# Issue order and planner numbers of a fused sliding-window attention and SiLU layer: loads booked at measured landing times, batch 1's k and q split, one copy moved to GpSimd

## Chip, cores and metric

One core of one Trainium2 chip. The time is device microseconds (us) of one execution. The span in the profile is about 1.8 us shorter than that time. The kernel before takes 323.43 us (median of three runs, 322.89 to 325.09). This is an already tuned kernel: TensorE is busy for 95% of the span, so the question is about 2 us in the first 60.

## The reference

Two stages, float32 in and out. Heads 0 to 3 look at the last 32 positions ("plain", p in the names below), heads 4 to 7 at every fourth of the last 128 ("dilated", d in the names).

```python
# q, k, v: (8, 8, 576, 64); w_in: (512, 2048); w_out: (2048, 512)
scores = scale * np.matmul(q, k.transpose(0, 1, 3, 2))
mask_plain = (rel >= 0) & (rel < 32)
mask_dil = (rel >= 0) & (rel < 32 * 4) & (rel % 4 == 0)
masks = np.stack([mask_plain if h < H // 2 else mask_dil for h in range(H)], axis=0)
attn = softmax(np.where(masks, scores, -1e9))            # cut: written out in the reference
x = np.matmul(attn, v).transpose(0, 2, 1, 3).reshape(B * S, H * D)   # 4608 x 512
h = x @ w_in
return (h * (1.0 / (1.0 + np.exp(-h)))) @ w_out
```

## The kernel before

The kernel computes batch after batch of attention on TensorE and puts the two matmuls of the second stage (h and y in the profile) between its pieces. The order of instructions is made while the kernel is being built, by a small planner: every piece of work is a step with an estimated duration on TensorE, estimated durations on VectorE or ScalarE, and a list of what it waits for. A step that reads loaded data waits for a landing time out of a table. The planner always takes a step that is ready by its own clock. On the chip each engine then takes its instructions in that order; where the table was wrong, TensorE stands in front of an instruction whose data aren't there, with ready work behind it.

```python
HOP = 0.12                      # from the end on one engine to the start on the next, us
# landing times by batch, us
AT_DIL = {0: 7.6, 1: 33.5, 2: 53.0}     # k, q for the "td" transposes (heads 4-7)
AT_PLAIN = {0: 11.0, 1: 33.5, 2: 53.0}  # k, q of heads 0-3
AT_VRAW = {0: 11.8, 1: 35.5, 2: 55.0}
AT_VP = {0: 14.3, 1: 45.0, 2: 58.0}
AT_REST = 16.0
AT_V1 = (17.6, 19.8)
AT_WIN = [18.5, 21.0, 23.5, 26.0]       # four chunks of w_in
AT_WOUT = [38.0, 40.5, 47.5, 50.0]      # four quarters of w_out
# ... cut
for f0 in range(0, DFF, FC):            # all these loads go through one queue, issued by GpSimd
    nc.gpsimd.dma_start(out=w_in16[:, :, f0 : f0 + FC], in_=wi[:, :, f0 : f0 + FC])
issue_nat(1, 0, H)                      # k and q of batch 1, all eight heads
issue_vraw(1)
for f0 in range(0, NFF, 4):
    if f0 == NFF // 2:
        issue_vp(1)                     # v of batch 1, behind two quarters of w_out
    nc.gpsimd.dma_start(out=w_out16[:, f0 : f0 + 4], in_=wo[:, f0 : f0 + 4])
# ... cut: best() gives a copy to VectorE or ScalarE, whichever the plan says ends it first
def best(dve, act):
    ends = {e: max(plan.now, plan.free[e]) + us for e, us in (("DVE", dve), ("ACT", act))}
    return ("DVE", dve) if ends["DVE"] <= ends["ACT"] else ("ACT", act)
# ... cut: one group of h, four matmuls for 128 columns of w_in
def l1(ring, f):
    h = (ps_x if ring == "x" else ps_h).tile([P, GT], F32, tag=ring, name=f"h_{g}_{f}")
    for c in range(HP):
        nc.tensor.matmul(h[:, :w], w_in16[:, c, f * P : (f + 1) * P], x_g[:, c],
                         start=(c == 0), stop=(c == HP - 1))
    # ... cut: tanh on ScalarE, then gT = (tanh + 1) * h on VectorE
```

The softmax here doesn't subtract the row's maximum and nothing guards it: scores larger than these inputs give would overflow.

## Time and profile before

| kernel before | |
|---|---|
| time, median of three | 323.43 us |
| span of the profiled run, mean granted clock | 321.2 us, 0.988 |
| TensorE busy | 304.2 us |
| of it between 20 and 40 us | 15.04 us, clock 0.84 |
| longest wait of TensorE after the start | 3.6 us, for k and q of batch 1, until 36.70 us |
| load booked for 33.5 us by the planner, landed | 36.57 us |

The names in the profile: td are the transposes of k and q of heads 4 to 7, nat is where k and q land, s are scores, av_p and av_d the products with v, h and y the two matmuls of the second stage. A group of h is four 256-column matmuls in the stage that matters here. The granted clock is the share of its full speed that TensorE was given; at 0.50 it runs at half speed. The prediction shows the lines.

### The profile page before, as it was taken

The page shows a single profiled execution, that of the slowest core. Times are in us where ns is not written, and L with a number is a line of the kernel's source. Part 1 is how long each engine was busy: PE and PEld are TensorE (multiplying, and loading weights), DVE is VectorE, ACT ScalarE, POOL GpSimd, SP SyncE. Part 2 cuts the span into 40 slices and gives each one's busy share as a digit, 9 for nine tenths or more (in the row PEclk, how much of TensorE's full clock was granted, in tenths as well). Part 3 has the DMA queues.
Part 4 walks back from the last instruction along what each step waited for, and adds up shares of the span by engine and source line. Part 5 has one row for each costly group of instructions (what it writes and reads, how often), then busy time and mean ns, then how long its engine had stood idle before and what let it go on. Part 6 is the DMA issues. An engine that isn't in the chain of part 4 may idle for free.

```text
span 321.2 us, 6143 instructions
## 1 busy us (share of the span) xinstructions
PE 304.2 (95%) x2402; PEld 156.4 (49%) x2402; DVE 198.6 (62%) x496; ACT 164.8 (51%) x299; POOL 54.0 (17%) x87
## 2 busy tenths in 40 slices
PE   1989599999999999999999999999999999999994
PEld 1658466555545444444454455445444444444442
DVE  7479488789878788753796578658651553255000
ACT  6557286677665365453654464556352453355111
POOL 8952624002700005004100410000000000000000
PEclk9998799999999999999999999999999999999999
DMA  7999999996999739998999799952270000100221
GB/s 89 152 194 192 197 191 192 194 214 126 161 208 207 144 94 156 210 209 183 181 216 185 157 183 156 261 123 70 69 166 33 34 35 33 65 35 0 78 87 65
DMA packets 106629, 44.51 MB, mean 139 GB/s; under 512 B 73320, under 2 KB 101992, under 8 KB 106600
## 3 DMA queue, kind: packets, MB, share of 16 engines
q0 software_dynamic: 48464, 19.92, 53.4%
q1 hardware_dynamic: 52952, 14.75, 25.5%
q10 hardware_dynamic: 5184, 9.44, 8.5%
q8 instruction: 19, 0.31, 0.4%
q14 instruction: 10, 0.08, 0.1%
HBM read 39.84 MB, written 18.28 MB: 181 GB/s over the span
## 4 chain that ended last, share of the span: by engine, by line
PE 83%; DMA 7%; POOL 3%; DVE 2%; ACT 2%; issue 1%; ACTq 0%; POOLq 0%
PE y L884 38%; PE h L851 36%; DMA nat<-in_q_dram 5%; PE s L599 3%; DMA vp<-in_v_dram 2%; PE av_d L646 2%; PE av_p L646 2%; DVE oD L650 1%; POOL nat L128 1%; PE td L505 1%; ACT ob L895 1%; ACT probs L608 0%; DVE probs L617 0%; PE ta L480 0%; POOL nat L117 0%
## 5 line engine op out<-in xcount | busy, mean ns | idle before, releaser
L884 PE MATMUL y<-w_out,gT 128*128 128x512 f16 x576 | 138.1, 379 | 0.0
L862 DVE SCALAR_TENSOR_TENSOR gT<-th,h 128x512 f16<-128x512 f32 (+1 forms) x160 | 98.9, 629 | 58.6 <-ACT th L860 58.3
L860 ACT ACTIVATE th<-h 128x512 f32<-128x512 f32 (+1 forms) x160 | 88.6, 556 | 80.6 <-PE h L851 73.3
L851 PEld LDWEIGHTS <-w_in 128*128 128x128 f16 x640 | 59.2, 99 | 54.0 <-issue 1.7
L884 PEld LDWEIGHTS <-gT 128*128 128x128 f16 x576 | 54.0, 98 | 60.0
L851 PE MATMUL h<-xR,w_in 128*128 128x512 f16 x320 | 77.2, 379 | 0.2 <-DVE gT L862 0.2
L851 PE MATMUL h<-xA,w_in 128*128 128x512 f16 (+1 forms) x320 | 66.9, 345 | 0.6 <-ACT probs L612 0.6
L608 ACT ACTIVATE probs<-s 128x768 f16<-128x768 f32 (+2 forms) x46 | 36.0, 782 | 21.6 <-PE s L599 19.9
L895 ACT ACTIVATE ob<-y 128x512 f32<-128x512 f32 x36 | 21.5, 597 | 41.8 <-PE y L884 41.7
L650 DVE TENSOR_TENSOR oD<-av_d,rcps 72x256 f16<-72x256 f32 x64 | 26.9, 421 | 2.2
L646 PEld LDWEIGHTS <-probs 128*128 128x128 f16 x448 | 21.7, 99 | 13.2 <-DVE probs L617 1.4
L650 DVE TENSOR_TENSOR oP<-av_p,rcps 96x256 f16<-96x256 f32 x48 | 20.2, 421 | 1.6
L384 POOL COPY fence<-kqT 128x1 f16<-128x1 f16 x10 | 1.8, 190 | 95.4 <-DMA kqT<-kq_s 95.4
L617 DVE TENSOR_TENSOR probs<-probs,mask_p 128x768 f16<-128x768 f16 x21 | 11.6, 554 | 8.4 <-ACT probs L608 8.4
L646 PE MATMUL av_d<-vd,probs 128*128 128x65 f16 x256 | 14.5, 198 | 0.5 <-DVE oD L650 0.3
L617 DVE TENSOR_TENSOR probs<-probs,mask_d 128x576 f16<-128x576 f16 (+1 forms) x23 | 11.9, 516 | 4.0 <-ACT probs L608 3.0
L646 PE MATMUL av_p<-vp,probs 128*128 128x65 f16 x192 | 13.1, 194 | 0.7 <-ACT probs L612 0.5
L649 DVE RECIPROCAL rcps<-av_d 72x4 f32<-72x4 f32 x64 | 11.0, 171 | 3.3 <-PE av_d L646 3.1
L649 DVE RECIPROCAL rcps<-av_p 96x4 f32<-96x4 f32 x48 | 8.3, 174 | 7.3 <-PE av_p L646 6.8
L163 POOL DMA_DIRECT2D vraw<-in_v_dram x16 | 10.8, 678 | 8.6 <-DVE gT L862 2.2
L176 POOL DMA_DIRECT2D vp<-in_v_dram x7 | 10.0, 1428 | 3.9 <-PE h L851 1.8
L522 PE MATMUL td<-ident,xR 96*128 96x96 f16 x8 | 1.9, 276 | 6.8 <-DMA xR<-in_q_dram 6.8
(96 smaller groups left out, 158.7 us busy)
## 6 DMA issues: line engine op xcount, KB each, us to landing
out_dram<-ob ACTq DMA_DIRECT2D x36, 256.0 KB, 2.0
kq_s<-in_k_dram POOLq DMA_DIRECT2D x5, 576.0 KB, 10.7
kq_s<-in_q_dram POOLq DMA_DIRECT2D x5, 576.0 KB, 13.2
vp<-in_v_dram POOLq DMA_DIRECT2D x7, 384.0 KB, 8.5
w_in<-in_moe_w_in_dram POOLq DMA_DIRECT2D x4, 512.0 KB, 9.9
w_out<-in_moe_w_out_dram POOLq DMA_DIRECT2D x4, 512.0 KB, 14.1
vraw<-in_v_dram POOLq DMA_DIRECT2D x8, 224.0 KB, 5.9
x_s<-oP SPq DMA_DIRECT2D x10, 144.0 KB, 2.6
```

What stands on the lines that cost most here:

```text
L163: nc.gpsimd.dma_start(out=vraw[p0 : p0 + m1 - m0, ab].rearrange("p h r d -> p h (r d)"), in_=src[m0:m1],)
L176: nc.gpsimd.dma_start(out=vps[b % NV][:, :, :D], in_=v_win(b * H * S - W, HN * NB, QB * D))
L608: nc.scalar.activation(p2, both[:, :, :n], AF.Exp, scale=scale)
L617: nc.vector.tensor_tensor(p2, p2, mk, ALU.mult)
L646: nc.tensor.matmul(a[:, i, : D + 1], lhs(i), rhs(i), start=True, stop=True)
L649: nc.vector.reciprocal(rcp[:n], a[:n, :, D : D + 1])
L650: nc.vector.tensor_tensor(o, a[:n, :, :D], rcp[:n, :, None].broadcast_to([n, HN, D]), ALU.mult)
L851: nc.tensor.matmul(h[:, :w], w_in16[:, c, f * P : (f + 1) * P], x_g[:, c], start=(c == 0), stop=(c == HP - 1),)
L860: nc.scalar.activation(th[:, :w], h[:, :w], AF.Tanh, scale=0.5)
L862: nc.vector.scalar_tensor_tensor(gTs[g][:, f, :w], th[:, :w], 1.0, h[:, :w], ALU.add, ALU.mult)
L884: nc.tensor.matmul(y, gTs[g][:, f, tb * P : (tb + 1) * P], w_out16[:, f], start=(f == 0), stop=(f == NFF - 1),)
L895: nc.scalar.activation(ob, y, AF.Copy, scale=0.5)
```

## The change

The intent: the planner is told when loads land on the chip and how long instructions really take from start to start, so that it doesn't order work behind data that are late. The landing times now come from a running sum over the order of issue, so order and table can't drift apart. Four parts:

- **Loads.** Order and landing times come from one list. k and q of batch 1 are split, heads 4 to 7 (d1) first. The v load of batch 1 (v1) goes one place earlier, ahead of the second quarter of w_out. The new table books d1 for 32.5 us, p1 for 36.2, w_in for 21.15 to 28.8, w_out for 40.15 to 50.4; the times booked for batches 0 and 2 change too.
- **GpSimd copy.** One copy of v (batch 0, second half) moves from ScalarE to GpSimd (c0).
- **Lean.** The copies of batch 0 go to ScalarE if VectorE would end less than 0.3 us sooner.
- **Costs.** HOP and the estimated durations change by 0.01 to 0.12 us, and the step that copies v no longer names VectorE as its engine.

```diff
+    ORDER = "k0 r0 v0 w0 w1 c0 w2 w3 d1 p1 r1 o0 v1 o1 o2 o3".split()
+    LOAD_US = {"w": 2.55, "o": 2.55, "d": 3.7, "p": 3.7, "r": 1.4, "v": 2.6, "k0": 0.9, "r0": 1.2, "v0": 2.0, "c0": 0.0}
+    AT_W0 = 14.5
 ... (the fixed issues of before are taken out)
+    at = AT_W0
+    for what in ORDER:
+        kind, n = what[0], int(what[1:])
 ... (w, o, k0, r0, v0 issue the loads of before)
+        elif what == "c0":
+            nc.gpsimd.tensor_copy(vds[0][:, 1, :, :, :D], vraws[0][:, 1])
+        elif kind == "d":
+            issue_nat(n, HN, H)
+        elif kind == "p":
+            issue_nat(n, 0, HN)
 ... (r, v)
+        at += LOAD_US[what if n == 0 and kind in "krvc" else kind]
+        AT[what] = at
-    HOP = 0.12
+    HOP = 0.18
+    LEAN = 0.3
-    AT_DIL = {0: 7.6, 1: 33.5, 2: 53.0}
+    t2 = at
+    AT_DIL = {0: 6.7, 1: AT["d1"], 2: t2 + 7.0}
 ... (the other tables in the same way)
-    AT_WIN = [18.5, 21.0, 23.5, 26.0]
-    AT_WOUT = [38.0, 40.5, 47.5, 50.0]
+    AT_WIN = [AT[f"w{n}"] for n in range(4)]
+    AT_WOUT = [AT[f"o{n}"] for n in range(4)]
-            return ("DVE", dve) if ends["DVE"] <= ends["ACT"] else ("ACT", act)
+            return ("DVE", dve) if ends["DVE"] + LEAN * (b == 0) <= ends["ACT"] else ("ACT", act)
-            step = best(0.44, 0.58)
+            step = best(0.37, 0.58)
 ... (a dozen more durations in the same way)
+            if b == 0 and ab == 1:
+                return                     # this copy of v is GpSimd's
```

More of the change, by code (lines that the diff above doesn't have):

```diff
@@ L202 @@
     issue_vp_first(0)
-    issue_part(k, MA, M, nat_of(0, "rest"), 0, H)
-    issue_vraw(0, (1,))
-    issue_vp_first(1)
     nc.vector.tensor_scalar(band, band, 1.0, BIG, ALU.subtract, ALU.mult)
@@ L224 @@
     wi = moe_w_in.rearrange("(c p) f -> p c f", p=P)
-    for f0 in range(0, DFF, FC):
-        nc.gpsimd.dma_start(out=w_in16[:, :, f0 : f0 + FC], in_=wi[:, :, f0 : f0 + FC])
     wo = moe_w_out.rearrange("(c p) m -> p c m", p=P)
-    issue_nat(1, 0, H)
-    issue_vraw(1)
-    for f0 in range(0, NFF, 4):
-        if f0 == NFF // 2:
-            issue_vp(1)
-        nc.gpsimd.dma_start(out=w_out16[:, f0 : f0 + 4], in_=wo[:, f0 : f0 + 4])
+    AT = {}
+    at = AT_W0
+    for what in ORDER:
+        kind, n = what[0], int(what[1:])
+        if kind == "w":
+            nc.gpsimd.dma_start(
+                out=w_in16[:, :, n * FC : (n + 1) * FC], in_=wi[:, :, n * FC : (n + 1) * FC]
+            )
+        elif kind == "o":
+            nc.gpsimd.dma_start(
+                out=w_out16[:, 4 * n : 4 * n + 4], in_=wo[:, 4 * n : 4 * n + 4]
+            )
+        elif what == "k0":
+            issue_part(k, MA, M, nat_of(0, "rest"), 0, H)
+        elif what == "r0":
+            issue_vraw(0, (1,))
+        elif what == "v0":
+            issue_vp_first(1)
+        elif what == "c0":
[4 more added lines that the diff above has]
+            issue_nat(n, 0, HN)
+        elif kind == "r":
+            issue_vraw(n)
+        else:
+            issue_vp(n)
+        at += LOAD_US[what if n == 0 and kind in "krvc" else kind]
+        AT[what] = at
     def third_batch():
@@ L317 @@
     plan = Plan()
-    AT_DIL = {0: 7.6, 1: 33.5, 2: 53.0}
-    AT_VRAW = {0: 11.8, 1: 35.5, 2: 55.0}
-    AT_PLAIN = {0: 11.0, 1: 33.5, 2: 53.0}
-    AT_VP = {0: 14.3, 1: 45.0, 2: 58.0}
-    AT_CAST = 64.0
-    AT_REST = 16.0
-    AT_V1 = (17.6, 19.8)
-    AT_WIN = [18.5, 21.0, 23.5, 26.0]
-    AT_WOUT = [38.0, 40.5, 47.5, 50.0]
+    t2 = at
+    AT_DIL = {0: 6.7, 1: AT["d1"], 2: t2 + 7.0}
+    AT_PLAIN = {0: 11.3, 1: AT["p1"], 2: t2 + 7.0}
+    AT_VRAW = {0: 12.2, 1: AT["r1"], 2: t2 + 8.6}
+    AT_VP = {0: 14.5, 1: AT["v1"], 2: t2 + 11.4}
+    AT_CAST = t2 + 18.0
+    AT_REST = AT["k0"]
+    AT_V1 = (max(AT["r0"] + 1.2, 18.0), AT["v0"])
+    AT_WIN = [AT[f"w{n}"] for n in range(4)]
+    AT_WOUT = [AT[f"o{n}"] for n in range(4)]
     readers = {}
@@ L487, in trans_a @@
             ):
-                step = best(us + 0.04, us)
+                step = best(us, us)
                 yield step
@@ L495, in trans_b @@
                 nc.tensor.transpose(tps[:, r], pairs["q"][:, hp, r], ident[:MA, :MA])
-            step = best(0.44, 0.40)
+            step = best(0.47, 0.40)
             yield step
@@ L525, in trans_d0 @@
                     )
-            step = best(0.41, 0.52)
+            step = best(0.40, 0.52)
             yield step
@@ L555, in trans_a0 @@
                         )
-            step = best(0.55, 0.48) if nm == "k" else best(0.76, 0.68)
+            step = best(0.47, 0.42) if nm == "k" else best(0.68, 0.56)
             yield step
@@ L614, in scores @@
                 return
-            yield "DVE", 0.12 + n / 960
+            yield "DVE", 0.07 + n / 960
             mk = mk.rearrange("p a c -> p (a c)")[:, None, :].broadcast_to([P, 2, n])
@@ L619, in paired @@
         def paired(key):
-            step = best(0.42, 1.0)
+            step = best(0.335, 0.95)
             yield step
@@ L633, in vd_of @@
         def vd_of(ab):
-            step = best(0.42, 1.0) if pe_path else ("DVE", 0.42)
+            if b == 0 and ab == 1:
+                return
+            step = best(0.335, 0.95) if pe_path else ("DVE", 0.335)
             yield step
@@ L647, in av @@
             n = o.shape[0]
-            yield "DVE", 0.50
+            yield "DVE", 0.545
             nc.vector.reciprocal(rcp[:n], a[:n, :, D : D + 1])
@@ L691, in x_p @@
             dst = x_b[:, : HP // 2, QB * j : QB * (j + 1)]
-            step = best(0.22, 0.30)
+            step = best(0.17, 0.22)
             yield step
@@ L705, in x_d @@
             for hp in range(HP // 2):
-                step = best(0.40, 0.40)
+                step = best(0.365, 0.36)
                 yield step
@@ L792, in attention @@
             elif kind == "V":
-                st = Step(lambda ring, a=a: vd_of(*a), 0.0, (), [AT_V1[0] if b == 0 and a[0] else at_vraw], ("DVE",))
+                st = Step(lambda ring, a=a: vd_of(*a), 0.0, (), [AT_V1[0] if b == 0 and a[0] else at_vraw], ())
             elif kind == "P":
@@ L860, in l1 @@
             nc.scalar.activation(th[:, :w], h[:, :w], AF.Tanh, scale=0.5)
-            yield "DVE", 0.11 + w / 960
+            yield "DVE", 0.06 + w / 960
             nc.vector.scalar_tensor_tensor(
```

## The prediction

> **What bounds the kernel now.** I read the page first: busy shares, the 40 slices, the list of groups.
>
> ```profile
> PE 304.2 (95%) x2402; PEld 156.4 (49%) x2402; DVE 198.6 (62%) x496; ACT 164.8 (51%) x299; POOL 54.0 (17%) x87
> ...
> PE   1989599999999999999999999999999999999994
> ...
> PEclk9998799999999999999999999999999999999999
> ```
>
> TensorE is busy 95% of the span. The holes are in slices 1, 3 and 5 (8.03 us each), the last one at the tail, and in two of the slices between 16 and 40 us the granted clock drops as well. So I looked at who TensorE waited for, then at stretches of 20 us.
>
> ```profile
> PE td L522 <- DMA xR<-in_q_dram: 6.8, 1, 6.8
> PE td L505 <- DMA nat<-in_q_dram: 3.6, 1, 3.6
> ...
> PE h L851 <- ACT probs L612: 0.6, 1, 0.6
> PE av_p L646 <- ACT probs L612: 0.5, 1, 0.5
> ```
>
> ```profile
> 20.00:40.00 20.00, 15.04 (x151) 12.59 (x151) 13.44 (x41) 10.31 (x27) 8.35 (x11) 0.84 1.41 197
> 40.00:60.00 20.00, 19.40 (x247) 12.67 (x245) 17.41 (x57) 13.99 (x36) 5.40 (x7) 0.99 1.86 189
> ...
> 80.00:100.00 20.00, 20.00 (x181) 9.86 (x179) 16.53 (x43) 12.27 (x21) 6.04 (x9) 1.00 1.54 186
> ```
>
> The columns are the stretch, its length, then busy time of PE, PEld, DVE, ACT and POOL, the granted clock, the DMA share and GB/s. From 80 us on TensorE is full (20.00 of 20.00), and later stretches lose 0.2 us in all until the tail. Nothing can be won there by waiting less. The first 6.75 us precede any change. What is left is 20 to 62 us: 4.96 us idle up to 40 us, 0.6 us up to 60 us and 0.3 us after it. The timeline of TensorE shows the one large hole, and stretches cut at the holes show the clock (the figure after POOL's).
>
> ```profile
> 32.94 0.21 PE L505 MATMUL td<-ident,nat 96*128 96x96 f16 x1
> 36.70 0.93 PE L505 MATMUL td<-ident,nat 96*128 96x96 f16 x11 [3.56 <-DMA nat<-in_q_dram]
> 37.43 1.05 PE L851 MATMUL h<-xA,w_in 128*128 128x256 f16 x4
> ```
>
> ```profile
> 23.20:26.70 3.50, 3.47 (x31) 2.85 (x32) 3.09 (x11) 1.60 (x5) 0.98 (x2) 0.51 1.25 206
> 26.70:33.20 6.50, 6.45 (x60) 5.57 (x58) 6.10 (x17) 5.54 (x16) 2.56 (x3) 1.00 1.64 182
> 33.20:36.70 3.50, 0.00 (x0) 0.03 (x1) 0.34 (x1) 0.32 (x1) 1.18 (x3) 1.00 1.44 197
> 36.70:40.30 3.60, 3.60 (x33) 3.06 (x34) 2.39 (x7) 1.02 (x2) 2.59 (x4) 0.53 1.27 209
> ```
>
> The hole is the wait for k and q of batch 1 (all eight heads), which the kernel planned for 33.5 us and which landed at 36.57 us by the chain of waits. Behind it the granted clock is 0.50 until about 40.2 us: four 256-column matmuls take 0.85 us from start to start there, and 0.46 us in the run from 26.2 to 33 us. The same happens from 23.2 to 26.7 us, behind three short holes (0.63, 0.50, 0.28 us).
>
> **What the Trainium skill says.** "TensorE: Matmul & The Clock Gate", part 1, says that the clock halves after an idle window of some 3.4 us of a free-running counter and comes back after a busy one. The trace agrees in size: 0.50 for about 3.5 us, twice. The first time no single hole is 3.4 us long, so a window that is only partly busy is enough here (1.4 us idle of about 3.4). "GPSIMD Engine Reference", section 4.1, calls one-input copies on GpSimd roughly line-rate, and section 1 gives 1.2 GHz: an estimate of 1024 / 1.2 GHz = 0.85 us, with overhead about 1 us, for the moved copy of 128x1024. The trace before has no GpSimd copy of that size; ScalarE took 1.05 us for it and VectorE 0.41 to 0.53 us. Section 1 there also says that GpSimd shares its SBUF interface with VectorE; no run so far shows what that costs here.
>
> **The change, part by part.** I compared the instruction lists of the two builds.
>
> (1) Loads. GpSimd issues the same bytes in nearly the same order: four w_in chunks, k and q of batch 1, v, w_out. But k and q of batch 1 are split: heads 4 to 7 (which the td transposes need) come first, in four issues, heads 0 to 3 in another four. Four more issues at about 0.7 us each (the nat issues took 0.63 to 0.84 us) on a GpSimd that was waiting on landings anyway: no cost on the path. The queue drains in order: w_in chunk 3 lets a GpSimd issue go at 29.51 us, the q load lands at 36.57. With half the bytes the first half lands about half way, 29.4 + 3.6 = 33.0 us, the second about 36.6 us. w_out has the same bytes ahead of it as before, so its quarters land as now: issued at 26.42, 29.51, 33.47, 36.36 with 13.3 to 14.5 us to landing, so about 40.5, 43.5, 47.5 and 50.7 us; one v load now comes ahead of the second, which moves that to about 45.5.
>
> (2) What TensorE does before td. In the old order 18 groups of four h matmuls precede td, in the new one 14. Those four take 4 x 0.46 = 1.8 us, so TensorE comes to td at 33.0 - 1.8 = 31.2 us if all else stays, and up to 32.3 us if the early stage is worse by a microsecond. It then waits for 33.0. The hole shrinks from 3.56 to between 0.7 and 2 us, and td itself starts at about 33.1 instead of 36.7. The gain is 3.6 us minus the 1.8 us of h matmuls that now come afterwards, so 1.8 us, plus what is saved in clock.
>
> (3) Clock. If the hole is short enough, the half-speed stretch behind it goes: 3.5 us at half speed are 1.75 us of work lost. I give that even odds. So 1.8 to 3.5 us at this point.
>
> (4) What limits that gain. From td to the fourth quarter of the first y tile the new order holds 24 td transposes (1.0 us), 18 h groups (8.1), six score sets (1.8), the other transposes (1.6), 32 av matmuls (1.6) and three y quarters (2.6): 16.7 us of TensorE. 33.0 + 16.7 = 49.7 us, but the last w_out quarter lands at 50.7 us, so it starts at about 51.2 us, with the clock penalty or without. Before, this quarter starts at 52.66 us with one h group and one score set (0.75 us) fewer behind it. So 53.4 - 51.2 = 2.2 us.
> VectorE is the check: from the first td copy to the last gT of group 1 the new list has 19 gT (6.6 us by their spacing of 0.345), seven normalisations (3.8), mask products (2.1), transposed copies (3.5), pair copies and the rest (1.5): 17.5 us. From 33.3 us that ends at 50.8, or about 53 with the idle time of before; it ended at 55.8 before. So VectorE allows 2 to 3 us too.
>
> (5) The small parts. The first copies lean to ScalarE: three of the four td copies go there, but ScalarE has its eight L221 copies until 7.84 us, so the scores of batch 0 start about 0.2 us later. The GpSimd copy of v takes 1.05 us from ScalarE at 19.08 us, at a time when w_in is already queued well ahead: it delays the next w_in issue to about 18 us, and that chunk's turn in the queue comes at 23.9. An h group now stands ahead of a score set at about 20 us and will wait there for the first w_in chunk (at 21.0 us), about 1 us instead of 0.63; the av wait on ScalarE stays at about 0.5 us. All of this lies ahead of the wait at td and is swallowed by it, unless it comes to over 0.8 us. I book it at zero.
> (6) New costs in the planner only change interleaving later on, where TensorE is full. Zero, give or take 0.5 us.
>
> Sum: 323.43 - 2.2 = 321.2 us.
>
> **The rivals.** (a) The hole only moves: TensorE waits at td, then for w_out, and VectorE (17.41 busy of 20 us between 40 and 60 us) becomes the bound; the new plan gives it more of the ta copies (1.5 us). For it: VectorE is nearly full from 45.5 to 55 us already (9.10 of 9.50). Against it: it was idle from 33.5 to 37.2 us and need not be. It makes 322.5 to 323.5. (b) Both half-speed stretches vanish and all holes close: 5.9 us idle and 3.5 us of clock, 9.4 us at most, 314 us. Against it: w_out's landing at 50.7 us, which the change doesn't bring forward, and the first w_in chunk at 21 us. Even a part of it, say 4 us, needs loads that land earlier than now. (c) The GpSimd copy holds up the queue, because it waits for its v load and all loads behind it wait too. GpSimd reaches it at about 15.4 us; its load had landed by 16.8, since the issue at 16.78 needed that landing. If it took 4 us instead of 1, the queue would still hold w_in until 23.9. It makes 321.5 to 323.
>
> **Range and chances.** The three ways to the gain give 1.8, 2.2 and 2 to 3 us; rival (a) takes it to 0.5, the better clock to 3.5 to 4. With the scatter of the runs before (322.89 to 325.09) I take 319.6 to 322.8. Faster by over 2% means below 316.96 us, 6.5 us of the 9.4 that exist at all: 0.03. Slower by over 2% would need a new stall of 6 us in a stage that is full: 0.01.
>
> **What would show it.** Right: td of batch 1 starts at about 33 us behind a hole of 0.7 to 2 us; the fourth y quarter starts at about 51.2 us; from 80 us on TensorE is full as before and all is shifted by about 2 us; GpSimd's copy takes about 1 us and no w_in chunk lands later. Wrong: k and q of heads 4 to 7 land at 35 us or later (the split issues cost queue time), or holes of over 1 us appear between 40 and 60 us behind VectorE (then rival (a)), or the clock stays at 1.00 throughout and the time is below 319.6 (then the y quarter was not bound by w_out).

## The result, and the profile after

Four runs each: 320.23 us (319.8 to 321.11) against 323.36 us. Ratios here are the mean time of one kernel's fast runs over the mean of the other's fast runs in the same rounds, which isn't quite the ratio of the medians; this one is 0.9897, 95% interval 0.9855 to 0.9939. A second set on another chip, 14 runs against 61, gives 320.08 against 322.28 us, ratio 0.9937 (0.9913 to 0.9961): 2.0 to 2.2 us. That set is the better one, and I use it below. The changed kernel is faster, by less than 1%.

The page of the changed kernel (busy times; then TensorE and its granted clock in 40 slices of 7.99 us):

```profile
PE 303.2 (95%) x2402; PEld 155.7 (49%) x2402; DVE 197.0 (62%) x493; ACT 164.3 (51%) x300; POOL 58.2 (18%) x92
...
PE   1969989999999999999999999999999999999994
...
PEclk9975999999999999999999999999999999999999
```

The hole of slice 5 is gone. The hole of slice 3 has stayed, and the clock of the slice behind it has fallen to half. The waits of TensorE (what waited for what: us in all, times, longest) say the same:

```profile
PE td L546 <- DMA xR<-in_q_dram: 6.9, 1, 6.9
PE h L877 <- DMA w_in<-in_moe_w_in_dram: 2.8, 1, 2.8
PE y L910 <- DMA w_out<-in_moe_w_out_dram: 0.6, 2, 0.4
```

The 3.6 us for k and q of batch 1 are gone (td waits 0.2 us once, at 59.20 us, for batch 2). In their place the first group of h now waits 2.8 us for the first w_in chunk; before, it waited 0.6 us, for ScalarE. The timeline of TensorE (start, us, instruction, in brackets the idle time ahead of it) shows where:

```profile
18.74 0.30 PE L623 MATMUL s<-kqD 64*128 64x72 f16 x8
21.81 1.03 PE L877 MATMUL h<-xA,w_in 128*128 128x256 f16 x4 [2.77 <-DMA w_in<-in_moe_w_in_dram]
...
34.45 0.68 PE L529 MATMUL td<-ident,nat 96*128 96x96 f16 x12
42.38 1.02 PE L910 MATMUL y<-w_out,gT 128*128 128x512 f16 x4 [0.40 <-DMA w_out<-in_moe_w_out_dram]
...
52.67 1.02 PE L910 MATMUL y<-w_out,gT 128*128 128x512 f16 x4
```

td starts at 34.45 us with no wait, against 36.70. The last two lines are the first and the fourth quarter of the first y tile; each quarter needs its own quarter of w_out. Now the stretches (length; busy PE, PEld, DVE, ACT, POOL; granted clock; DMA share; GB/s), first those of the prediction, then two around the new hole:

```profile
20.00:40.00 20.00, 17.37 (x176) 13.91 (x177) 13.30 (x41) 10.47 (x29) 11.62 (x17) 0.74 1.29 181
40.00:60.00 20.00, 18.59 (x229) 11.93 (x229) 17.78 (x60) 12.66 (x30) 5.67 (x8) 1.00 1.53 198
80.00:100.00 20.00, 20.00 (x192) 10.12 (x189) 16.89 (x42) 13.48 (x24) 8.11 (x11) 1.00 1.40 170
```

```profile
16.80:20.20 3.40, 2.13 (x40) 1.20 (x39) 1.73 (x6) 2.37 (x6) 3.40 (x6) 1.00 1.24 184
20.20:30.50 10.30, 8.07 (x68) 5.75 (x69) 4.82 (x17) 3.43 (x10) 3.06 (x6) 0.50 1.30 201
```

Between 20 and 40 us TensorE is busy 2.3 us longer than before, but at a clock of 0.74 instead of 0.84: ten microseconds at half speed, against 3.5 and 3.6 before. Busy time and work are two things here. To compare work I counted, for several moments of each trace, which matmuls had yet to start, and took 0.216 us for one of 512 columns, 0.109 for 256 and 0.035 for the small ones. It is an estimate from the traces' own spacings at full clock. Work still to do, us:

| at (us) | before | changed, 1st profile | changed, 2nd profile |
|---|---|---|---|
| 33 | 273.8 | 277.0 | 274.7 |
| 40 | 272.2 | 270.7 | 269.2 |
| 62 | 252.6 | 251.5 | 249.7 |
| 100 | 215.7 | 214.2 | 212.2 |
| span | 321.2 | 319.4 | 317.4 |

The changed kernel comes to 33 us behind the old one (by 3.2 and 0.9 us of work): it stood in front of w_in and ran cold. It overtakes between 33 and 40 us, where the old one stood for 3.6 us and then ran at half speed. From 40 us on it leads by 1.1 to 1.5 us in one profile and by 2.9 to 3.5 in the other.

What holds TensorE from there on is w_out. The issues of its four quarters (first and last start) and the time from issue to landing, in the first profile:

```profile
L235 POOL DMA_DIRECT2D w_out<-in_moe_w_out_dram x4: 749/772/780, 33.5 to 37.1; - x4
DMA to landing us min/median/max: 8.8/12.6/15.3
```

By the trace's landing events the quarters are there at 42.34, 47.38, 49.96 and 52.48 us. The first quarter of y starts at 42.38, after a wait of 0.40 us, the second at 47.43, after 0.23. From there it is 5.24 us of TensorE to the fourth, which starts at 52.67 without a wait, but only 0.19 us after its load. In the kernel before, the last quarter of w_out had landed at 50.86 us, and TensorE came to it at 52.66, 1.8 us late. TensorE keeps the order that it was given: had it been faster ahead of 42 us, it would only have waited longer for the first quarter. So neither the hole at w_in nor the cold stretch behind it reached the end here.

### The profile page after: what moved, and what is told of

It is laid out like the page before. It is cut to its first block, busy times and chain, and to the rows that moved or that the text cites. A ratio compares the mean times of both kernels' runs of the same rounds, so it can differ in the third digit from the quotient of the medians.

```text
span 319.4 us, 6150 instructions
## 1 busy us (share of the span) xinstructions
PE 303.2 (95%) x2402; PEld 155.7 (49%) x2402; DVE 197.0 (62%) x493; ACT 164.3 (51%) x300; POOL 58.2 (18%) x92
## 4 chain that ended last, share of the span: by engine, by line
PE 82%; DMA 10%; POOL 4%; DVE 1%; issue 1%; ACT 0%; POOLq 0%
PE y L910 37%; PE h L877 36%; DMA nat<-in_q_dram 5%; PE s L623 3%; DMA w_out<-in_moe_w_out_dram 3%; DMA w_in<-in_moe_w_in_dram 3%; PE av_d L672 2%; PE av_p L672 2%; POOL vp L188 1%; POOL nat L131 1%; POOL vraw L166 1%; DVE oD L676 0%; POOL xR L131 0%; PE td L529 0%; PE xp L714 0%
## 5 line engine op out<-in xcount | busy, mean ns | idle before, releaser
L632 ACT ACTIVATE probs<-s 128x768 f16<-128x768 f32 (+2 forms) x47 | 36.2, 771 | 12.8 <-PE s L623 10.2
```

The costliest lines, as they stand in the source:

```text
L632: nc.scalar.activation(p2, both[:, :, :n], AF.Exp, scale=scale)
```

## The experiments

Twelve runs in three calls (the first is the changed kernel again); runs of one call share a chip and the runs of the kernel before. Where an edit is "to the changed kernel" it is that kernel plus the lines shown. All gave the right result, and all profiled runs were fast ones. The theory on record at the start was that of the prediction; the rivals were the clock, the GpSimd copy, and a hole that only moves.

| run | median us (runs) | ratio to before (95%) |
|---|---|---|
| after_again | 320.08 (14) | 0.9937 (0.9913 to 0.9961) |
| loads_only | 320.30 (22) | 0.9947 (0.9926 to 0.9968) |
| costs_only | 321.80 (22) | 0.9984 (0.9965 to 1.0004) |
| no_pool_copy | 320.26 (16) | 0.9928 (0.9903 to 0.9953) |
| before, first call | 322.28 (61) | |
| warm_hole | 318.99 (9) | 0.9916 (0.9883 to 0.9950) |
| warm_both | 318.86 (6) | 0.9899 (0.9864 to 0.9934) |
| no_split | 320.13 (10) | 0.9942 (0.9912 to 0.9973) |
| w0_early | 320.38 (13) | 0.9941 (0.9915 to 0.9966) |
| before, second call | 322.45 (25) | |
| td_time_only | 323.53 (22) | 1.0049 (1.0028 to 1.0070) |
| times_only | 323.61 (21, of them 6 slow, which the ratio leaves out) | 1.0018 (0.9994 to 1.0042) |
| no_lean | 320.21 (22) | 0.9955 (0.9934 to 0.9976) |
| warm_no_pool | 319.76 (22) | 0.9936 (0.9917 to 0.9955) |
| before, third call | 322.26 (73) | |

### The changed kernel once more

No edit.

> The changed kernel once more, for another profile and for the spread. Its first profile showed half clock from 20.2 to 30.5 us (mean clock 0.984) while three other executions had 0.989 to 0.995 and were only 0.8 to 1.3 us shorter. Theory L (loads: the weights' landing caps the early stage): the span stays between 318 and 319.5 us whatever the clock, and with a better clock there are longer waits for loads. Theory C (the clock phase is the gain): span follows the clock one to one, about 3 us between clock 0.984 and 0.995. Ratio to before expected 0.990.

Measured: 320.08 us, and a second profile (span 317.4 us). Its timeline at the same places:

```profile
21.20 0.61 PE L877 MATMUL h<-xA,w_in 128*128 128x256 f16 x4 [2.52 <-DMA w_in<-in_moe_w_in_dram]
...
31.78 0.93 PE L529 MATMUL td<-ident,nat 96*128 96x96 f16 x12
40.35 1.02 PE L910 MATMUL y<-w_out,gT 128*128 128x512 f16 x4 [0.66 <-DMA w_out<-in_moe_w_out_dram]
...
50.59 1.02 PE L910 MATMUL y<-w_out,gT 128*128 128x512 f16 x4
```

Nearly the same hole, 2.5 us, stands in front of w_in, but here the clock stayed down for a much shorter time: over 20 to 33 us it was 0.87, against 0.61 in the first profile. td starts 2.7 us earlier (0.6 of that because the first w_in chunk let TensorE go earlier), and the fourth y quarter 2.1 us earlier. It is tempting to put the 2.1 us down to the clock. But the loads differ as well:

```profile
L235 POOL DMA_DIRECT2D w_out<-in_moe_w_out_dram x4: 747/751/774, 31.8 to 35.5; - x4
DMA to landing us min/median/max: 8.5/12.2/15.0
```

The quarters of w_out landed at 40.30, 45.31, 47.87 and 50.53 us, each 2.0 to 2.1 us earlier than in the first profile. In both profiles TensorE waits for the first (0.66 us here) and the second (0.31, until 45.35), and the fourth y quarter starts 5.24 us later (here 0.06 us after its own load). Nothing shows that TensorE delayed them: the queue was 0.6 us apart at the first w_in chunk, 1.1 at the fourth and 1.4 at the first k load of batch 1 (31.31 and 29.91 us), and the next issue came 0.55 us after that landing in both. So the 2.1 us are those of the loads, and what the clock cost ahead of them was taken up by the waits. The waits grew from 0.6 to 1.0 us with the better clock, as theory L said, though its range of spans (318 to 319.5 us) was too narrow: the 14 runs have 317.2 to 320.5.

The other kernels with the new loads (below) say the same. In nine of the ten profiles the span ends 266.8 to 267.6 us after the last quarter of w_out has landed, whether that was at 49.91 us (no_pool_copy, span 317.1 us) or at 53.61 (no_lean, 320.8); in no_split it is 268.3. Over the ten, the span's correlation with that landing is 0.95, with the mean clock (0.984 to 1.000) 0.07. Over the 14 runs of the changed kernel alone the span does fall as the mean clock rises, by 0.22 us for each 0.001 (correlation -0.60). That isn't shown to be the clock's doing: the other eight kernels with the new loads have anything from -0.68 (no_lean) to 0.43 (warm_both) here. A late queue could lengthen both the cold stretch behind w_in and the wait for w_out; only the profiled runs show landings, so this stays open.

### The loads alone, and the costs alone

```diff
 loads_only, to the kernel before
+    ORDER = "k0 r0 v0 w0 w1 w2 w3 d1 p1 r1 o0 v1 o1 o2 o3".split()
 ... (the loop over ORDER and the new landing tables; old costs and HOP, no lean, no c0)
```

> The kernel before with the new load order, the split of k and q of batch 1, and the new landing times in the planner; engine costs, HOP and copies as before, no GpSimd copy, no lean. Theory L (my prediction): this is nearly the whole gain, ratio 0.990 to 0.993. Theory P (the planner's engine spacings make the gain): ratio 0.997 to 1.0.

```diff
 costs_only, to the kernel before
-    HOP = 0.12
+    HOP = 0.18
+    LEAN = 0.3
 ... (all new durations; old order, old landing tables, no c0)
```

> The kernel before with the new engine costs, HOP 0.18 and the lean to ScalarE, but old load order and old landing times, no GpSimd copy. Theory L: the hole of 3.5 us at td stays, ratio 0.998 to 1.002. Theory P: ratio 0.990 to 0.994.

Measured: loads_only 0.9947, the whole gain within the intervals; costs_only 0.9984, nothing that the interval separates from nil. costs_only has the old hole (its timeline):

```profile
37.18 1.04 PE L506 MATMUL td<-ident,nat 96*128 96x96 f16 x11 [3.86 <-DMA nat<-in_q_dram]
```

So order and landing times suffice for the gain, and costs and lean without them don't give it. loads_only also shows the landing of the split load, since td waits for it there (1.14 us, to 32.19 us): 0.8 us before the 33.0 us that I had predicted. In warm_hole this wait ended at 31.80 us, in warm_no_pool at 32.68, in no_lean at 33.50, so this landing scatters by 1.7 us.

### Without the GpSimd copy

```diff
 no_pool_copy, to the changed kernel
-    ORDER = "k0 r0 v0 w0 w1 c0 w2 w3 d1 ..."
+    ORDER = "k0 r0 v0 w0 w1 w2 w3 d1 ..."
-            if b == 0 and ab == 1:
-                return
```

> The changed kernel without the GpSimd copy: the second half of v of batch 0 goes to ScalarE or VectorE as before. In the changed kernel the first w_in chunk let TensorE go at 21.8 us instead of 21.1. If the copy holds back the loads queued behind it, that chunk lands at about 21.1 us here and the second and later ones earlier too; time then within 0.3% of the changed kernel (theory L, loads cap later too) or up to 0.7 us faster. If the copy is what brings the gain, it is 1 to 2 us slower.

Measured: 0.9928 against 0.9937 with the copy, no difference. GpSimd's timeline of the changed kernel has the copy and its wait:

```profile
16.30 1.04 POOL L245 COPY vd<-vraw 128x1024 f16<-128x1024 f16 x1 [1.05 <-DMA vraw<-in_v_dram]
```

1.04 us, as estimated. It does put off the issues of the third and fourth w_in chunk, from about 15.3 to 17.3 us, which TensorE doesn't wait for. Whether it puts off the first chunk, I can't say: the first h group was released at 20.95 to 21.81 us in runs with the copy, and at 20.71 to 21.37 in runs without it.

### Filling the hole: does the clock count?

If the clock behind the hole costs time, dummy matmuls in the hole must win time; if the end is set by w_out's landing, they win nothing. They write to the PSUM tile that the h group then overwrites (start=True), so the result stays right.

```diff
 warm_hole, to the changed kernel, in l1 ahead of the matmuls
+            if g == 0 and f == 0:
+                for _ in range(14):
+                    nc.tensor.matmul(h[:, :384], ident, mask_p.rearrange("p a c -> p (a c)")[:, :384], start=True, stop=True)
 warm_both: the same, and ahead of all else
+    nc.vector.memset(warm, 1.0)
+    for _ in range(44):
+        nc.tensor.matmul(wps[:, :P], warm, warm, start=True, stop=True)
```

> The changed kernel with 14 useless 384-column matmuls into the first h tile, ahead of its real ones (which overwrite it), so that TensorE is busy while it waits 2.5 to 2.8 us for the first w_in chunk (14 x 0.16 us = 2.3 us at full clock). Theory C (half clock behind that hole costs time): mean clock rises from about 0.990 to 0.997 or more and, by the slope of 0.22 us per 0.001 over the 14 executions of the changed kernel, 1 to 2 us are gained, ratio to before about 0.988. Theory L (loads and VectorE cap the stage): the clock rises but the time stays within 0.4 us of the changed kernel, ratio 0.992 to 0.995.

> As the one before, and 44 useless 128-column matmuls from about 1.4 us on, before the first load is there, so that the first transposes run at full clock too (they take twice the time until 13 to 16 us now). They end before the first load lands at 6.8 us (44 x 0.107 = 4.7 us). Theory L: TensorE reaches the first w_in chunk earlier and waits longer, nothing gained over the run with the filled hole alone. Theory C: another 1 us or more.

Measured: warm_hole 318.99 us, warm_both 318.86. The timeline of warm_hole at the hole:

```profile
18.66 2.45 PE L878 MATMUL h<-mask_p,ident 128*128 128x384 f16 x14
20.94 0.60 PE L880 MATMUL h<-xA,w_in 128*128 128x256 f16 x4
```

The clock was 0.998 to 1.000 in all nine runs of warm_hole. Median against median it is 1.1 us below the changed kernel (other call, other chip), and the intervals of the two ratios overlap. Taken alone, the direction is that of the clock theory. But the landing is a rival: in the profiled run the last quarter of w_out landed at 49.91 us, as in that of no_pool_copy, which has a span of 317.1 us at a mean clock of 0.995 against 317.3 at 1.000 here. And the fourth y quarter, with td reached 0.9 us earlier than in the second profile of the changed kernel, starts at 50.57 us as it did there (50.59), behind a wait of 0.58 us for VectorE (gT) that isn't there in that profile. Two of the nine runs took 321.7 and 321.9 us at full clock. So a gain from filling the hole isn't shown.

Filling the idle start as well (warm_both) adds nothing that can be told apart. Nor was it the warm start that it was meant to be: in its profile the clock is at half again from 8.8 to 15.6 us (0.74 over 6.7 to 20 us).

> The best two together: the changed kernel with the hole in front of the first w_in chunk filled with useless matmuls (alone about 1.1 us faster than the changed kernel) and without the GpSimd copy (first w_in chunk at 20.7 instead of 21.2 to 21.8 us, alone no difference in time). If the copy's delay of the first w_in chunk counts once the clock is up: ratio 0.986 to 0.990, about 0.5 us better than the filled hole alone. If not: 0.989 to 0.993. The 14 matmuls may now be 0.3 us too many.

The edit is that of warm_hole and that of no_pool_copy together. Measured: 0.9936, no better than warm_hole's 0.9916 and no better than no_pool_copy's 0.9928. Its mean clock was 0.992 to 1.000 in 22 runs, so the higher clock didn't bring the time down here; in its profile (span 319.8 us) TensorE waits 0.91 us for the last quarter of w_out, which landed at 52.63. The best medians are those of warm_hole and warm_both, about 1 us below the changed kernel, unproven at this number of runs.

### Without the split

```diff
 no_split, to the changed kernel
-    ORDER = "... w2 w3 d1 p1 r1 o0 v1 o1 o2 o3"      # "d": 3.7, "p": 3.7
+    ORDER = "... w2 w3 n1 r1 o0 v1 o1 o2 o3"         # "n": 7.4
-        elif kind == "d": issue_nat(n, HN, H)
-        elif kind == "p": issue_nat(n, 0, HN)
+        elif kind == "n": issue_nat(n, 0, H)
```

> The changed kernel with k and q of batch 1 loaded for all heads at once (four issues), planned landing 36.2 us for both uses. My prediction gives the whole gain to the split: then td waits till about 36 us or is planned there, and the time goes back to that of the kernel before, ratio 0.998 to 1.002. Rival: the planner, now told the right landing time, fills the time ahead of td with h matmuls, and the ratio stays below 0.996: then it is the right landing time and not the split.

Measured: 0.9942. The gain is there without the split. td now comes as late as in the kernel before, but the hole doesn't:

```profile
36.84 0.63 PE L527 MATMUL td<-ident,nat 96*128 96x96 f16 x11 [0.96 <-DMA nat<-in_q_dram]
```

Told that the load lands at 36.2 us, the planner puts 22 groups of h ahead of td, where the old table had put 18, and TensorE works until the data are nearly there. My reason for the gain, "half the bytes land half way", isn't needed for it. It could be that the right time alone is enough; that is the next pair.

### The right times in the old order

```diff
 td_time_only, to the kernel before
-    AT_DIL = {0: 7.6, 1: 33.5, 2: 53.0}
+    AT_DIL = {0: 7.6, 1: 36.6, 2: 53.0}               # AT_PLAIN in the same way
 times_only, to the kernel before
+    AT_DIL = {0: 7.6, 1: 36.6, 2: 57.5}               # AT_PLAIN in the same way
+    AT_VRAW = {0: 11.8, 1: 38.5, 2: 59.0}
+    AT_VP = {0: 14.3, 1: 45.7, 2: 61.8}
+    AT_WIN = [21.0, 23.5, 26.1, 29.2]
+    AT_WOUT = [40.5, 43.5, 47.5, 50.7]
```

> The kernel before with one number changed in two tables: the planned landing of k and q of batch 1, 36.6 us as the trace shows instead of 33.5. Loads, copies and engine costs untouched. The planner now puts 25 groups of h matmuls ahead of td instead of 18. The run without the split suggests that the right landing time is enough: then the 3.6 us hole at td all but goes and the ratio is 0.993 to 0.996. If the new load order as such (not the split) makes the gain, the ratio stays at 0.998 or more, because the h matmuls that now come first are missing as fill further on.

> The kernel before with all planned landing times of the first 60 us set to those its trace shows (k and q of batch 1 36.6, v 38.5 and 45.7, w_in 21.0 to 29.2, w_out 40.5 to 50.7, batch 2 57.5 to 61.8); loads, copies and engine costs untouched. If the landing times in the planner are the whole gain: ratio 0.991 to 0.995, no slower than with the one number. If the load order adds something: 0.996 or more here against 0.9947 of the run with order, split and times together.

Measured: 1.0049 and 1.0018. Neither gains; td_time_only loses. The timeline of times_only:

```profile
36.96 0.63 PE L505 MATMUL td<-ident,nat 96*128 96x96 f16 x11 [0.98 <-DMA nat<-in_q_dram]
...
48.26 1.02 PE L884 MATMUL y<-w_out,gT 128*128 128x512 f16 x4 [2.38 <-DMA w_out<-in_moe_w_out_dram]
```

The hole at td has shrunk to 0.98 us, and one of 2.38 us has opened in front of w_out. In td_time_only TensorE waits 2.7 us there. This is the rival "the hole only moves", though it isn't what cost the time. By the count of work still to do, times_only was ahead at 40 us (268.4 against 272.2), still ahead at 62 (251.3 against 252.6) and 80 us (233.8 against 235.6), and behind at 100 us (216.2 against 215.7): between 80 and 100 us TensorE waits 1.0 us for VectorE and 0.5 us for a v load, and is busy for 18.56 of the 20 us. So ordering by right times isn't enough by itself. loads_only and no_split both hold the gain, and both have, beside right times, the v load of batch 1 ahead of w_out's second quarter, which times_only hasn't. That is a candidate, but not the only one: they also share the times booked for batch 0 and for w_out (45.3 us for its second quarter, against 43.5). It wasn't tried by itself, and loads_only has the split and no_split the new costs besides; which of these it takes stays open. The new order with the old times wasn't tried either. Six of the 21 runs of times_only were slow ones (326.3 to 328.2 us), against two of 73 of the kernel before; why isn't shown.

What the kernels with the gain have in common is that TensorE comes to the fourth y quarter in time: it starts it 0.04 to 0.66 us after the last quarter of w_out has landed, against 1.8 us in the kernel before, 2.5 in costs_only and 2.7 in td_time_only. times_only has this too (0.35 us) and loses it again between 80 and 100 us.

### The first w_in chunk earlier

```diff
 w0_early, to the changed kernel
-    ORDER = "k0 r0 v0 w0 w1 c0 ..."
+    ORDER = "k0 r0 w0 v0 w1 c0 ..."
```

> The changed kernel with the first w_in chunk issued ahead of the three v loads of batch 0 that come last (v0). The chunk should land about 2 us earlier, 19.2 to 19.8 us instead of 21.2 to 21.8, and the hole in front of the first h matmuls shrink from 2.5 us to under 1 us, while v0 lands at about 20. Theory L: all later loads land as before, so 0 to 0.5 us gained; theory C: less half clock too, 1 us or more gained.

Measured: 0.9941, no gain. TensorE no longer waits for w_in, but for the v load that was pushed back:

```profile
20.16 0.30 PE L672 MATMUL av_p<-vp,probs 128*128 128x65 f16 x4 [2.35 <-DMA vp<-in_v_dram]
```

Some 2.4 us ahead of 21 us are missing in either order; neither brings both loads in time.

### Without the lean

```diff
 no_lean, to the changed kernel
-    LEAN = 0.3
+    LEAN = 0.0
```

> The changed kernel with the lean of the first copies to ScalarE set to zero. I booked the lean at nothing. Expected: within 0.5 us of the changed kernel, ratio 0.991 to 0.996; if the lean matters, 1 us or more slower.

Measured: 0.9955 against 0.9937, intervals overlapping by more than half. No effect is shown.

## Why the prediction was right or wrong, point by point

The time was right (321.2 us, 2.2 us of gain, against 2.0 to 2.2 in the larger set and 3.1 in the first four runs). The cap by w_out, which gave the figure, held. The way to it was partly wrong, and it is luck that this didn't show: the wait for w_out took it up.

1. **The split brings k and q forward.** True as to time (31.8 to 33.5 us where td waited for it, 33.0 predicted), wrong as the cause: no_split has the gain too. Right times alone aren't enough either (td_time_only, times_only): the new order of the loads, or the other times booked with it, belongs to the cause. What they share, and what wasn't tried, is said with those runs.
2. **td at about 33.1 us behind a hole of 0.7 to 2 us.** There was no hole in either profile of the changed kernel, with td at 34.45 and 31.78 us. TensorE came late in the first, being cold, and the load was early in the second.
3. **The clock, at even odds.** The half-speed stretch behind td did vanish (clock 1.00 from 33 to 40 us in both profiles). What I left out is that a new one would come ahead of td: 10.3 us in the first profile. In these two profiles it cost nothing in the end (next item).
4. **The cap: the fourth y quarter at 51.2 us, "with the clock penalty or without", because w_out's last quarter lands at 50.7.** This held in substance: w_out sets the pace. TensorE waited for its first two quarters in both profiles, and the fourth y quarter came 5.24 us after the second, 0.06 and 0.19 us after its own load. The work of TensorE was right as well: 16.7 us predicted, 18.2 and 18.8 from td to this quarter, less waits of 1.35 and 1.8 us 16.9 and 17.0. What was wrong is "its quarters land as now", as a fixed time: 50.53 us in the second profile, but 52.48 in the first, and 49.91 to 53.61 over the ten profiles with the new loads. The sum needed a scatter there, and I had taken it only from the runs before.
5. **The early stage costs nothing, as the h group waits about 1 us.** It waited 2.8 and 2.5 us. Two things added up: TensorE was through with the last score set ahead of it at 19.0 and 18.7 us, 1.0 and 1.3 us sooner than I had it (20.0), and the first chunk let it go at 21.81 and 21.20 us, not 21.0. That is the term that I mis-sized, and it went beyond the 0.8 us that I had allowed. Nor was it "swallowed" at td, as I had put it: there is no wait at td left. The next wait down the line, for the first quarter of w_out, swallowed it.
6. **GpSimd copy, lean, costs: zero.** The copy took 1.04 us, as said; no_pool_copy, no_lean and costs_only show no effect.

Of the rivals, (b) "all holes close" didn't come near; (c) the copy as a brake isn't shown; (a) "the hole only moves" didn't happen to the changed kernel as a whole, but half of it did: from td to the first h group, and to the quarters of w_out. times_only shows it plainly.

The signs named for "wrong" did their work too: I had said that a full clock and a time below 319.6 us would mean that the y quarter wasn't bound by w_out. warm_hole, the same kernel but for the filler, at 318.99 us and full clock, is that case: its quarter started 0.66 us after the load, behind the 0.58 us for VectorE. In loads_only, no_split, no_lean and warm_no_pool TensorE waited for this load, 0.39 to 1.75 us.

## What to carry to other kernels

When the order of instructions comes from a planner, measured landing times belong in it, together with the order of the loads: one corrected number (td_time_only) only sent the wait to the next load and lost 0.5%. Follow an early slip down to the next wait for a load before you book it as lost: the one here, with its cold clock, ended in the wait for w_out. When spans scatter, look at the landing times next to the clock: over ten profiles the span went with the last landing of w_out, and not with the mean clock. And before a gain is put down to one part of a change, try the change without it: the most visible part, the split, wasn't needed.

## What the Trainium skill lacked or had wrong

- "TensorE: Matmul & The Clock Gate", part 1, gives half rate "after ≥1 idle window (~3.4µs)". Here a window only partly idle was enough: 2.13 of 3.40 us busy from 16.80 to 20.20 us, and the clock was at 0.50 just after. It stayed there for 10.24 us, though TensorE was busy for most of them. By the clock records the stretches at half clock last 3.41 us in eight kernels, 6.82 in warm_both and 10.24 here: one, two and three times the page's window. Further on the page has frequent short idles between groups of matmuls make the clock swing; how busy a window must be it doesn't say, and the runs don't settle it.
- "GPSIMD Engine Reference", section 4.1, calls one-input operations roughly line-rate. The copy of 128x1024 took 1.04 us, against 0.85 us by the estimate in the prediction, and against 1.05 us on ScalarE and 0.41 to 0.53 us on VectorE before: right, with 0.2 us more than the rate alone.
- No page that I read says how the profile's clock reads before its first record. In the kernel before, that record is a change to full clock at 16.38 us, and the profile gives 1.00 from the start; but the pair of 288-column matmuls at 9.60 us takes 0.59 us to the next instruction, at 17.38 us 0.35. In warm_both, whose record does have 0.50 at that point, the same pair takes 0.60 us at 9.64. So the start was cold, and mean clocks leave that out. The default at half rate that part 1 of the TensorE page gives fits this.
- No page that I read says how far the landings of one program's loads scatter: the last quarter of w_out landed between 49.91 and 53.61 us in the ten profiles with the new loads, issued by GpSimd between 35 and 37.2 us, and the span went with it. With changes of 1 us, that takes many runs.
